# A decode step of attention and MLP: VectorE's program on a block border, and eight more matmuls on TensorE

## The chip, the cores and the metric

One Trainium2 chip, of which one core runs the kernel. The metric is device time in microseconds of one execution; the time of a kernel is the median of its runs. In the profile PE is TensorE's matmuls, PEld its weight loads, DVE VectorE, ACT ScalarE, POOL GpSimd and SP the engine whose queue issues nearly all DMAs here.

## The reference

Eight tokens (one for each batch entry, 576 wide) go through two branches that a gate mixes. Attention has 32 query heads on 16 key/value heads of 128, over the last 2048 of 8192 cached positions:

```python
x = A_x
g = _sigmoid((x * gate_w).sum(-1, keepdims=True))
# a: attention
q = (x @ wq).reshape(B, Sq, Hq, Dh).transpose(0, 2, 1, 3)
k = jnp.repeat(k_cache[:, :, Sk - W:, :], rep, axis=1)
v = jnp.repeat(v_cache[:, :, Sk - W:, :], rep, axis=1)
scores = jnp.einsum("bhqd,bhkd->bhqk", q, k) * (Dh ** -0.5)
p = _softmax(scores, axis=-1)
o = jnp.einsum("bhqk,bhkd->bhqd", p, v)
a = o.transpose(0, 2, 1, 3).reshape(B, Sq, Hq * Dh) @ wo
# b: MLP
h = _gelu(jnp.einsum("bsd,df->bsf", _layernorm(x), w1) + b1)
b = jnp.einsum("bsf,fd->bsd", h, w2) + b2
return g * a + (1 - g) * b
```

All inputs are bf16. The K and V windows are 64 MiB each; with the weights the kernel reads 154 MB.

## The kernel before, in words

The whole kernel is a plan: every operation is put in with `add` or `dma` (an engine, a function that emits the instructions, what it waits for, an estimated cost), `P.schedule()` orders the operations of each engine by these estimates, and `P.emit` then writes one engine's program after the other, with semaphore waits where another engine's work or a DMA is needed. `deps` are waited for; `after` only sets the order. The instructions that the framework puts ahead of each engine's program are there before the first `emit`.

Work is staged by what the DMA queue of SP brings, in this order: `wq`, `w1`, then 16 units of K and V of 4 MiB each, alternating, through four slots of SBUF, and at the end `M0`, `W0`, `W1`, `M1` of the list `stream`: two thirds of `w2`, the two halves of `wo`, and the last third of `w2` in three pieces of 8, 3 and 1 rows of blocks. A load is issued when its slot is free.

For each unit VectorE turns K around in four transposes (L719), TensorE makes the scores in PSUM banks 0 to 3 (on top of a mask that four matmuls of the constants `mrow` and `mcol` write there), VectorE takes the maximum (L643), ScalarE the exponential (L647), VectorE and ScalarE lay the probabilities out in blocks, and TensorE multiplies them with V in a loop on registers (L188). Four units make a group, whose parts VectorE scales and adds; `sel_x` and `oT` then bring the group's output into the form in which `wo` takes it. The last unit's V product is in bank 0.

The output is gathered in bank 7 (`BK_ACC`). A group of matmuls into it is an `AccGroup` (L567): one pair of matmuls (L576) of 8 columns for each block of 128 rows of `wo` or `w2`, one for each half of the 576 output columns. `wo_chunk(i)` (L829) loads half of `wo` and makes the group `proj0` or `proj1` of 16 pairs; `m2_chunk` (L845) makes the groups of `w2`. The list `o_m2` holds them in the order of their making, and each has the one before it in its `after`, so TensorE takes them in the order of `stream`. At the end VectorE (L883) and ScalarE (L884) copy one half each out of bank 7, and two DMAs write the output.

`held_matmul` (L174) emits a matmul that uses the weights which the matmul before it loaded.

Of the kernel before, what the change touches and what calls it, by code (L numbers as in the profile page):

```python
# [38 lines left out]
class _Plan:  # L39
# [10 lines left out]
    def add(self, eng, fn, deps=(), name=None, cost=0.1, after=(), prio=0):  # L50
        op = _Op(eng, fn, deps, name, cost, after=after, prio=prio)
        op.idx = len(self.all)
        self.all.append(op)
        return op

    def dma(self, eng, fn, semkey, nbytes, deps=(), name=None, after=(), prio=0):
        op = _Op(eng, fn, deps, name, self.DMA_ISSUE, after=after, is_dma=True, dma_sem=semkey, nbytes=nbytes, prio=prio)
        op.idx = len(self.all)
        self.all.append(op)
        return op  # L60
# [113 lines left out]
def held_matmul(nc, e, out, lhsT, rhs, start=False, stop=True, skip=False, tile_size=(128, 128), tile_position=(0, 0)):  # L174
    return e.add_instruction(mybir.InstMatmult(  # L175
        name=nc.get_next_instruction_name(), engine=mybir.EngineType.PE,
        ins=[e.lower_ap(rhs), e.lower_ap(lhsT)], outs=[e.lower_ap(out)],
        start_tensor_calc=start, stop_tensor_calc=stop, is_transpose=False, bass_skip_group_check=skip,
        tile_size=tile_size, tile_position=tile_position, ldweights=False))
# [15 lines left out]
def build_kernel(nc, A_x, A_k_cache, A_v_cache, A_wq, A_wo, B_x, B_w1, B_b1, B_w2, B_b2, gate_w, out):  # L195
# [29 lines left out]
    with ExitStack() as es:  # L225
# [79 lines left out]
        def view(name, parts=128):  # L305
            o, n, dt = R[name]
            a = arena[0:parts, o // 2: o // 2 + (n * (2 if dt == BF else 4)) // 2]
            if dt == F32:
                a = a.bitcast(F32)
            return a  # L310
# [5 lines left out]
        mrow, mcol = view("mrow"), view("mcol")  # L316
# [34 lines left out]
        def slot(s):  # L351
            return RAW[:, s * DE:min((s + 1) * DE, ND * DE + WOR * D)]
# [8 lines left out]
        def col(i, parts=128):  # L361
# [3 lines left out]
        ps = es.enter_context(nc.psum_tensor("ps", [128, 8, 512], F32))  # L365
# [13 lines left out]
        add, dma = P.add, P.dma  # L379
# [4 lines left out]
                                                        fill=0.0, base=0, channel_multiplier=1), deps=[o_ones], name="ident", cost=0.3)  # L384
        o_idf = add("pool", lambda e: e.tensor_copy(idf8, ident[0:8, 0:8]), deps=[o_ident], name="idf8", cost=0.15)
        o_r8 = add("pool", lambda e: e.tensor_copy(r8.rearrange("p (k b) -> p k b", b=8), bass.AP(arena_f, offset=foffs("idf8"), ap=[[AST // 2, 8], [0, 16], [1, 8]])),
                   deps=[o_idf], name="r8", cost=0.2)
# [5 lines left out]
                                                     fill=0.0, base=0, channel_multiplier=-1), deps=[o_ones], name="maskR", cost=0.8, prio=-1)  # L393
        o_mrow = add("pool", lambda e: e.affine_select(out=mrow, in_=zeros_bf, pattern=[[0, 8], [1, 8], [0, 2]], compare_op=ALU.is_equal,
                                                       fill=-BIG, base=0, channel_multiplier=-1), deps=[o_z], name="mrow", cost=0.3, prio=-1)
        o_mcol = add("pool", lambda e: e.affine_select(out=mcol, in_=ones_bf, pattern=[[0, 16], [1, 8], [0, 4]], compare_op=ALU.is_equal,
                                                       fill=0.0, base=0, channel_multiplier=-1), deps=[o_ones], name="mcol", cost=0.8, prio=-1)
# [23 lines left out]
        for s in range(2):  # L421
            o_xz.append(add("dve", (lambda s=s: lambda e: e.tensor_copy(xz[:, s, :].rearrange("p (k z) -> p k z", z=2)[:, :, s], x_sb[:, 512:576]))(),  # L422
                            deps=dx + [o_xz0], name="xz%d" % s, cost=0.12))
# [12 lines left out]
        for s in range(2):  # L436
            o_yz.append(add("dve", (lambda s=s: lambda e: e.tensor_copy(yz[:, s, :].rearrange("p (k z) -> p k z", z=2)[:, :, s], y_bf[:, 512:576]))(),
                            deps=[o_y, o_yz0], name="yz%d" % s, cost=0.12))
# [91 lines left out]
        for he in range(4):  # L530
            def fn(e, he=he):
                src = bass.AP(ps, offset=BK_SEL * 512 + 8 * he, ap=[[PST, 128], [1, 8], [32, 32]])
                return e.activation(out=q4[:, he, :, :], in_=src, func=ACTF.Copy)
# [49 lines left out]
        NU = NG * NT  # L583
# [14 lines left out]
        exp_done, sp_done, pv_done, mx_done = {}, {}, {}, {}  # L598
# [4 lines left out]
        def take_slot():  # L603
            n = n_slot[0]
            n_slot[0] += 1
            return (1, 2, 0, 3)[n % ND]
# [222 lines left out]
        def wo_chunk(i):  # L829
            s = ND if i == 0 else take_slot()  # L830
            dst = slot(s)[:, 0:WOR * D].rearrange("p (j c) -> p j c", j=WOR)
            src = A_wo.rearrange("(p j) c -> p (j c)", j=WOP)[:, WOR * D * i:WOR * D * (i + 1)]
            d = dma("sp", lambda e: e.dma_start(slot(s)[:, 0:WOR * D], src), "s%d" % s, WOR * 128 * D * 2, deps=slot_free[s], name="d_wo%d" % i, after=last_dma[-1:])
            last_dma.append(d)
            mms = [(oT[:, WOR * i + j, :], dst[:, j, :]) for j in range(WOR)]
            slot_free[s] = [AccGroup("proj%d" % i, mms, [oT_done[n] for n in range(NG)] + [d], cost=2.4, prio=2, after=o_m2[-1:]).op]
            o_m2.append(slot_free[s][0])

        o_m2, o_bias = [], []

        def bias(i):
            d = dma("act", lambda e: e.dma_start(b2_sb, B_b2.partition_broadcast(8)), "b2", 8 * D * 2, name="d_b2", after=[d_b1])
            o_bias.append(AccGroup("m2_b", [(ob[:, 0:8], b2_sb), (ob[:, 8:16], b2_sb)], [d, o_obl, o_obh], cost=0.6, after=[o_hp]).op)
# [20 lines left out]
        for kind, i in stream:  # L864
            {"K": k_item, "V": v_item, "W": wo_chunk, "M": m2_chunk, "B": bias}[kind](i)
# [21 lines left out]
        add("sp", lambda e: e.sem_inc(eng_sems["sp"], 1), deps=fin, name="final_wait", cost=0.05)  # L887

        P.schedule()
        for eng, handle in (("sp", nc.sync), ("act", nc.scalar), ("pool", nc.gpsimd), ("dve", nc.vector), ("pe", nc.tensor)):  # L890
            P.emit(eng, handle, eng_sems, dma_sems)

# [3 lines left out]
def bass_gated_mix__sliding_block_cached__mixer_channel_mlp__decode_kernel(  # L896
    nc: bass.Bass,
    A_x: bass.AP,
    A_k_cache: bass.AP,
    A_v_cache: bass.AP,  # L900
    A_wq: bass.AP,
    A_wo: bass.AP,
    B_x: bass.AP,
    B_w1: bass.AP,
    B_b1: bass.AP,
    B_w2: bass.AP,
    B_b2: bass.AP,
    gate_w: bass.AP,
    out: bass.AP,
):  # L910
    build_kernel(nc, A_x, A_k_cache, A_v_cache, A_wq, A_wo, B_x, B_w1, B_b1, B_w2, B_b2, gate_w, out)
# [28 lines left out]
```

## Time and profile before

| | before |
|---|---|
| median of 3 runs | 365.51 us (364.80 to 365.84) |
| the profiled execution | 365.76 us, of which the span from the first to the last instruction is 364.3 us |
| busy: PE, PEld, DVE, ACT, POOL | 293.8, 125.8, 237.3, 166.7, 26.4 us |
| DMA | 154.48 MB, mean 424 GB/s over the span |
| mean granted clock of TensorE | 0.963 |
| matmul instructions | 1944 |
| code fetched by DMA within the span | 8 packets of 16 KB (queue q8), 3 of 8 KB (queue q14) |

The page's strip of 40 slices gives the busy share of each engine over time, the granted clock (PEclk, in tenths of full speed) and the share of the 16 DMA engines that is busy. The chain of waits follows the last instruction back to what released it. The trace also keeps each DMA packet (start, length, size, queue), the landing events of each transfer, of which there are 16, one for each DMA engine, and the stretches of time in which each clock was granted. Times of single records count from the first instruction of the span.

### The profile page before, as it was taken

What the parts mean: (1) busy time and instruction counts of PE and PEld (TensorE: products, weight loads), DVE (VectorE), ACT (ScalarE), POOL (GpSimd) and SP (SyncE); (2) the same over time, 40 slices, a digit from 0 to 9 for tenths busy, and PEclk for the clock granted to TensorE, in tenths of its full rate; (3) what the DMA queues carried; (4) which work ended last, traced back from release to release, by engine and by line L of the source; (5) the groups of instructions that cost most, each with busy time, mean ns of one, the idle gap of its engine ahead of it and who ended that gap; (6) DMA issues with size and microseconds to landing.
All of it is one profiled execution on the core that took longest, in us unless ns stands there. A gap on an engine that the chain in (4) does not pass through costs nothing.

```text
span 364.3 us, 4853 instructions
## 1 busy us (share of the span) xinstructions
PE 293.8 (81%) x1944; PEld 125.8 (35%) x1420; DVE 237.3 (65%) x218; ACT 166.7 (46%) x122; POOL 26.4 (7%) x53
## 2 busy tenths in 40 slices
PE   0356544999999989999999798979797899979865
PEld 0201000253443524342525143423334160607643
DVE  0722976667768796858496868577585858396710
ACT  1012108373838483828383828281828365563000
POOL 9320070000010000000100000000000000003000
PEclk9976696999999999999999999999999999999998
DMA  8999999999999999999999999999999999999995
GB/s 348 433 428 412 457 407 454 407 457 407 457 412 453 425 439 428 431 435 428 446 417 444 417 450 414 457 412 450 410 453 417 447 423 439 425 439 425 432 418 208
DMA packets 6147, 154.48 MB, mean 424 GB/s; under 512 B 716, under 2 KB 884, under 8 KB 1272
## 3 DMA queue, kind: packets, MB, share of 16 engines
q1 hardware_dynamic: 6064, 154.28, 98.4%
q8 instruction: 8, 0.13, 0.1%
q10 hardware_dynamic: 72, 0.04, 0.1%
q14 instruction: 3, 0.02, 0.0%
HBM read 154.31 MB, written 0.01 MB: 424 GB/s over the span
## 4 chain that ended last, share of the span: by engine, by line
DMA 42%; DVE 36%; PE 13%; issue 7%; ACT 1%; ACTq 0%; POOL 0%
DMA arena<-in_A_k_cache_dram 32%; DVE arena L719 26%; DMA arena<-in_A_wo_dram 8%; PE ps L175 6%; DVE arena L643 4%; PE ps L188 2%; DMA arena<-in_gate_w_dram 2%; DVE arena L666 2%; PE ps L732 2%; PE ps L576 1%; PE ps L498 1%; DVE arena L795 1%; DVE arena L559 1%; DVE arena L554 0%; ACT arena L647 0%
## 5 line engine op out<-in xcount | busy, mean ns | idle before, releaser
L719 DVE STREAM_TRANSPOSE arena<-arena 128x2048 f32<-128x2048 f32 x64 | 143.3, 2281 | 14.4 <-DMA arena<-in_A_k_cache_dram 11.9
L175 PE MATMUL ps<-arena 128*128 128x512 bf16 (+3 forms) x524 | 132.2, 397 | 0.0
L672 ACT ACTIVATE arena<-arena 32x2048 bf16<-32x2048 bf16 x60 | 114.5, 1908 | 20.8 <-DVE arena L666 19.7
L188 PE MATMUL ps<-arena 128*128 x840 | 102.6, 275 | 3.4 <-issue 0.9
L188 PEld LDWEIGHTS ps<-arena 128*128 x840 | 81.7, 97 | 23.2 <-issue 10.1
L732 PE MATMUL ps<-arena 128*128 128x512 bf16 x128 | 51.0, 399 | 34.1 <-DVE arena L719 32.4
L732 PEld LDWEIGHTS ps<-arena 128*128 128x128 bf16 x128 | 12.4, 97 | 147.7 <-DVE arena L719 98.3
L644 ACT ACTIVATE arena<-arena 128x1 f32<-128x1 f32 x16 | 3.2, 203 | 114.3 <-DVE arena L643 114.3
L643 DVE TENSOR_REDUCE arena<-ps 128x1 f32<-128x2048 f32 x16 | 36.7, 2291 | 28.7 <-PE ps L175 28.7
L666 DVE STREAM_TRANSPOSE arena<-arena 128x1024 f32<-128x1024 f32 x15 | 18.7, 1245 | 37.5 <-ACT arena L647 37.5
L647 ACT ACTIVATE arena<-ps,arena 128x2048 bf16<-128x2048 f32 x16 | 40.6, 2535 | 0.5
L753 PE MATMUL ps<-arena 128*128 128x256 bf16 x184 | 25.3, 273 | 0.9 <-DMA arena<-in_A_v_cache_dram 0.9
L753 PEld LDWEIGHTS ps<-arena 128*128 128x128 bf16 x184 | 16.6, 100 | 13.3 <-issue 8.8
L576 PE MATMUL ps<-arena 128*8 128x288 bf16 (+1 forms) x140 | 11.1, 319 | 6.0 <-DMA arena<-in_A_wo_dram 5.1
L741 POOL MEMSET arena<- 128x4096 f32 x1 | 3.5, 3512 | 151.6 <-PE ps L175 151.6
L626 POOL COPY arena<-arena 32x64 bf16<-32x64 bf16 x16 | 3.7, 229 | 130.5 <-PE ps L175 122.9
L884 ACT ACTIVATE arena<-ps 8x288 bf16<-8x288 f32 x1 | 0.4, 401 | 27.5 <-PE ps L576 27.5
L449 PE MATMUL ps<-arena 8*128 8x8 bf16 x8 | 0.5, 170 | 15.0 <-DVE arena L422 10.2
L683 PE MATMUL ps<-arena 128*128 128x512 bf16 x16 | 6.5, 407 | 6.5 <-ACT arena L647 5.2
L576 PEld LDWEIGHTS ps<-arena 128*8 128x8 bf16 (+1 forms) x140 | 6.6, 95 | 11.1 <-DMA arena<-in_A_wo_dram 3.6
L795 DVE SCALAR_TENSOR_TENSOR arena<-ps,arena 128x128 f32<-128x128 f32 x28 | 9.3, 334 | 1.7 <-PE ps L753 1.3
L883 DVE CAST arena<-ps 8x288 bf16<-8x288 f32 x1 | 0.4, 445 | 14.1 <-PE ps L576 14.1
(103 smaller groups left out, 90.6 us busy)
## 6 DMA issues: line engine op xcount, KB each, us to landing
arena<-in_A_k_cache_dram SPq DMA_DIRECT2D x16, 4096.0 KB, 29.0
arena<-in_A_v_cache_dram SPq DMA_DIRECT2D x16, 4096.0 KB, 27.4
arena<-in_B_w_dram SPq DMA_DIRECT2D x1, 4608.0 KB, 23.7
arena<-in_A_wo_dram SPq DMA_DIRECT2D x2, 2304.0 KB, 31.1
arena<-in_A_wq_dram SPq DMA_DIRECT2D x1, 4096.0 KB, 13.4
arena<-in_B_w_dram SPq DMA_DIRECT2D x1, 3456.0 KB, 27.7
arena<-in_B_w_dram SPq DMA_DIRECT2D x1, 1152.0 KB, 22.6
arena<-in_B_w_dram SPq DMA_DIRECT2D x1, 576.0 KB, 24.6
```

The source lines that it names most:

```text
L175: return e.add_instruction(mybir.InstMatmult(name=nc.get_next_instruction_name(), engine=mybir.EngineType.PE, ins=[e.lower_ap(rhs), e.lowe ...
L188: return e.add_instruction(mybir.InstMatmult(name=nc.get_next_instruction_name(), engine=mybir.EngineType.PE, ins=[rhs, lhsT], outs=[e.low ...
L576: ins = e.matmul(ps[32 * j:32 * j + 8, BK_ACC, 0:JN], lhsT, rhs[:, JN * j:JN * j + JN], start=False, stop=True, skip_group_check=True, til ...
L643: mx = add("dve", lambda e: e.tensor_reduce(out=k(g, MX + x), in_=scores, axis=AXL.X, op=ALU.max), deps=[qk_unit[t]], name="mx%d" % t, cos ...
L647: ex = add("act", lambda e: e.activation(out=bass.AP(arena, offset=aoffs("P"), ap=[[AST, 128], [64, 32], [1, 2], [2, 32]]), in_=ps[:, 0:4, ...
L666: pc = add("dve", lambda e: e.transpose(view("PC").bitcast(F32), view("P").bitcast(F32)), deps=[ex] + (sp_done[t - 1][0] if t else [o_acc0 ...
L672: return e.activation(out=bass.AP(arena, offset=32 * a * AST + aoffs(home) + 64 * a, ap=[[AST, 32], [256, 32], [1, 64]]), in_=bass.AP(aren ...
L683: mm = e.matmul(*args, start=True, stop=False, skip_group_check=True) if n == 0 else held_matmul(nc, e, *args, start=True, stop=False, ski ...
L719: tr = add("dve", (lambda h=h, kb=kb, r2=r2: lambda e: e.transpose(bass.AP(arena_f, offset=foffs("KT") + kb * 2048, ap=[[AST // 2, 128], [ ...
L732: mm = e.matmul(*args, start=False, stop=True, skip_group_check=True) if rc == 0 else held_matmul(nc, e, *args, stop=True, skip=True)
L753: return e.matmul(dst, bass.AP(arena, offset=aoffs(home) + 256 * q + ee, ap=[[AST, 128], [2, 128]]), slot(s).rearrange("p (r k d) -> p r k ...
L795: fn = lambda e, src=src, w=w: e.scalar_tensor_tensor(out=X[:, g % 2, :], in0=src, scalar=w, in1=X[:, g % 2, :], op0=ALU.mult, op1=ALU.add)
```

## The change

Two things are added, and nothing is taken away.

In `wo_chunk`, behind `proj0`, TensorE gets an operation `fill`: eight matmuls of the mask's constants `mrow` and `mcol`, 128 by 128 by 512, into banks 1, 2 and 3 in turn, which nothing reads any more by then. The first loads the weights, the other seven hold them. `fill` goes into `o_m2`, so it stands between `proj0` and `proj1`. It depends on the last unit's exponential, which was the last reader of these banks.

Ahead of the emission VectorE gets an `addr_align(128, max_nops=0)`: the next instruction on it, the first of the kernel's own, is placed at a multiple of 128 instructions of 64 bytes (8 KB), and a branch leads over the gap in place of a row of no-operations.

```diff
@@ wo_chunk(i)
             slot_free[s] = [AccGroup("proj%d" % i, mms, [oT_done[n] for n in range(NG)] + [d], cost=2.4, prio=2, after=o_m2[-1:]).op]
             o_m2.append(slot_free[s][0])
+            if i == 0:
+                filler("fill", 8, o_m2[-1:])
 
         o_m2, o_bias = [], []
+
+        def filler(name, n, after):
+            def fn(e):
+                mm = None
+                for i in range(n):
+                    args = (ps[:, 1 + i % 3, :], mrow, mcol)
+                    mm = e.matmul(*args, start=True, stop=True, skip_group_check=True) if i == 0 else held_matmul(nc, e, *args, start=True, stop=True, skip=True)
+                return mm
+            o_m2.append(add("pe", fn, deps=[exp_done[NU - 1], o_mrow, o_mcol], name=name, cost=0.21 * n, after=after))
@@ ahead of the emission
         P.schedule()
+        nc.vector.addr_align(128, max_nops=0)
         for eng, handle in (("sp", nc.sync), ("act", nc.scalar), ("pool", nc.gpsimd), ("dve", nc.vector), ("pe", nc.tensor)):
             P.emit(eng, handle, eng_sems, dma_sems)
```

## The prediction

> **What bounds the kernel now.** I read the page first, then the chain of waits from its end backwards, then the busy time by stretches of the last 18 us, then the trace's single records of packets, landings and matmuls.
>
> ```profile
> PEclk9976696999999999999999999999999999999998
> DMA  8999999999999999999999999999999999999995
> ...
> q8 instruction: 8, 0.13, 0.1%
> ...
> q14 instruction: 3, 0.02, 0.0%
> ```
>
> The 16 DMA engines are full from the second slice to the last but one; no compute engine is. The granted clock is whole through the middle and dips in the last slice. Two queues carry nothing but code: 8 packets of 16 KB on q8 and 3 of 8 KB on q14. The end of the chain of waits (start, length, what):
>
> ```profile
> 327.60 29.48 DMA arena<-in_A_wo_dram
> 357.07 0.04 issue
> 357.12 5.29 PE ps L576 x56
> 362.43 0.45 DVE arena L883
> ```
>
> The second block of `wo` lands at 357.07; from there 56 matmuls, 28 pairs, run to the end. The busy time of the tail by stretches (length, then busy time and count of PE, PEld, DVE, ACT, POOL, then clock, DMA share, GB/s):
>
> ```profile
> 351.60:353.90 2.30, 2.13 (x32) 1.43 (x32) 0.00 (x0) 0.00 (x0) 0.00 (x0) 1.00 0.91 385
> 353.90:357.10 3.20, 0.00 (x0) 0.00 (x0) 0.00 (x0) 0.00 (x0) 0.00 (x0) 1.00 0.99 420
> 357.10:359.00 1.90, 1.88 (x20) 1.19 (x22) 0.00 (x0) 0.00 (x0) 0.00 (x0) 0.62 0.95 392
> 359.00:361.00 2.00, 2.00 (x22) 1.11 (x18) 0.00 (x0) 0.00 (x0) 0.00 (x0) 0.50 0.47 181
> 361.00:362.40 1.40, 1.39 (x22) 0.81 (x18) 0.00 (x0) 0.00 (x0) 0.00 (x0) 1.00 0.00 0
> ```
>
> `proj0` runs to 353.9, TensorE stands idle 3.2 us, and then works at half clock while the last data land. The four landings that feed the tail are at 357.07 (`wo`, 16 pairs), 359.82 (8 pairs), 360.87 (3) and 361.25 (1). The clock records put half clock from 357.57 to 360.99; starts of pairs are 0.1225 us apart at full clock and 0.240 at half. So the tail is 4 pairs full, 14 half, 10 full, and its last matmul ends at 362.39, 1.14 us after the last landing. Two things set the end: when the slowest DMA engine delivers, and the clock at which TensorE consumes.
>
> **The eight matmuls.** They stand on TensorE between `proj0` and `proj1`. What they wait for (ScalarE's last exponential, two constants from GpSimd) was over before 341, and the banks 1 to 3 that they write have no reader left, so they add no wait. TensorE is free at 353.7. The same kind of matmul, the held ones of the mask, takes 0.68 us for three in the chain of waits, so eight take 8 x 0.22 = 1.8 us, to 355.5. The 3.3 us of waiting for `wo` hides them; at half clock they would end near 357.2, and only what passes the landing of `wo` would be paid, up to 0.5 us.
>
> Do they hold the clock? The clock's changes all lie on one grid of 3.413 us. I took the busy share of TensorE in each cell: the cell 354.16 to 357.57 has 0.13 and is followed by half clock, as are cells with 0.11, 0.26 and 0.41; the lowest from 70 us on that kept full clock has 0.49 (279.1). With the filler that cell holds 1.39 us of it and 0.45 us or more of `proj1`: 1.84 of 3.41, 0.54, on the keeping side. The grid may lie otherwise in another run; the largest hole with the filler is then 349.9 to 351.7, which is there now too, and a cell around it has at worst 0.46, between the known rows. At full clock with the same landings: `proj1` 357.12 to 359.08, then 359.87 + 8 x 0.1225 = 360.85, 360.92 + 3 x 0.1225 = 361.29, the last pair done 0.29 us later, at 361.58. That is 0.81 us less. Now the landings, not the matmuls, set the end.
>
> The Trainium skill (TensorE: Matmul & The Clock Gate, Part 1) says that the clock falls back after at least one idle window of about 3.4 us. Taken at its word it speaks against the filler: the gap here is 3.27 us between matmuls, so nothing would be lost now and nothing won, 0 in place of 0.81 us. The clock of 0.50 after a cell that was 13% busy decides against that reading.
>
> Could the filler push TensorE over another code border? TensorE's fetches come at 336.64 and 351.32, 258 instructions apart. Behind the last there are 177 to the end; some 10 more stay below 258. No cost.
>
> **VectorE's start at a border.** A branch is added, and VectorE reaches it before 2.0 us, while its first work begins at 9.46, after the DMA of `gate_w`. Without that cover a wait for code would be paid in full, but even then not at once by the end: K and V loads land 27 to 29 us after issue and follow each other at 9.66 us, so the queue holds over 17 us of work. On that count I put the branch at nothing.
>
> What moves is where the borders lie, and each has a fetch. VectorE runs 47 of its recorded instructions before the 8 KB fetch at 61.25 and 178 before that at 284.76: 131 apart, a block of 128 within what its queue runs ahead. (The third 8 KB fetch, at 147.17, fits ScalarE.) Each fetch goes to one DMA engine: at 284.76 it starts as one 32 KB packet ends, takes 0.309 us, and the 32 KB packet behind it takes 1.744 instead of 1.213. That engine loses 0.84 us. The landing events (16 for each transfer, one for each DMA engine) show who it was: up to 279.45 the last five engines are within 0.12 us of each other; from the landing at 289.67 on, one engine is alone behind the rest, by 0.53 us, and is still 0.42 behind at 357.07 and 0.45 behind at 361.25. By its place in the row it is the one that the fetch at 61.25 had hit, and it was 0.42 from last before. So two fetches of VectorE on one DMA engine hold the last landings 0.42 us behind eight others, each hit once by a 16 KB fetch.
>
> With the program at a border, the next block is asked for at the start, before some 2 us, where the DMA engines are not yet full, and the one behind it 128 instructions on, which is VectorE's work at 202 to 207 us. One of the two hits moves to where nothing queues; the engine would then end 0.84 - 0.42 us ahead of the eight, and these set the landings. Bounds: 0 if the fetch falls on another late engine or the start still costs a place in the queue, at most 0.84 if the eight gained too, a loss of up to 0.84 if a hit is added to one of the eight. I take 0.42, the row's own distance. The Trainium skill (Runtime: NRT & Kernel Launch, Instruction fetch mechanics) calls the cost of crossing a block "mostly hidden"; by it this term would be 0, and the packet of 1.744 us speaks against that.
>
> **The sum.** Landings at 356.65, 359.40, 360.45, 360.83: the three pairs run 360.50 to 360.87, the last pair ends at 361.17. 362.39 - 361.17 = 1.22 us, of which 0.81 is clock and 0.41 fetch. The profiled execution took 365.76 us, of which 364.3 is span; it goes to 364.54. That execution is 0.25 above the median of the runs, 365.51. Taking the same 1.22 from the median gives 364.29, which I forecast as 364.3. The lowest run, 364.8, is about what the sum gives for a grid that happens to spare the tail (365.76 - 0.81 = 364.95); from such runs only the fetch's part comes off, to 364.4.
>
> **Rivals.**
> Only the clock: the code fetch hits a late DMA engine again. For it: eight engines wait at 0.42 to 0.57 us. Against it: both earlier hits were on one engine. 365.51 - 0.81 = 364.7.
> Only the fetch: the filler is too little for the gate. With landings 0.42 earlier the tail has 7 pairs full, 14 half, 7 full, ending at 362.01, so 365.51 - 0.38 = 365.1. For it: 0.54 is not far from 0.49, and activity may be weighed otherwise than I do. Against it: `proj0`'s cell, 0.62 busy with only 8 columns filled, kept the clock. If the alignment is also without effect, nothing changes: 365.5.
> Slower: the branch ends the reading ahead, so that VectorE meets each later border without its block. The one near 205 us is covered by the queue's 17 us. The last border then lies about 30 instructions behind VectorE's end, in the closing part behind the span, where nothing covers it. Its price I bound by the 1.93 us between the first two code packets of the trace's opening; it decides from 1.22 us on: 364.29 + 1.93 = 366.2, and without the clock's 0.81, 367.0. Against it: the trace shows a fetch at 365.64 and no wait in the span that either border explains. The Trainium skill (Runtime: NRT & Kernel Launch, Instruction fetch mechanics) states that a taken branch to a page outside the current two forces a fetch before execution goes on. The target here is the next block, and no run yet shows such a branch.
>
> **How the numbers follow.** Both parts 0.60; only the clock 0.17; only the fetch or nothing 0.13; slower 0.07; a gain beyond the sum 0.03. The range takes in the first two, most of the third, and downward the lowest run less the whole 0.84 us, 363.9: from 363.8 to 365.3. What a measurement of this kernel can tell from no change is about 0.3%, 1.1 us, so faster means below 364.4. The likeliest case, 364.3 to 364.5, sits on that line: most of it and the gain beyond count as faster, 0.52; its rest and the partial cases as the same, 0.42; slower 0.06.
>
> **What would show it.** A held matmul group of eight behind `proj0`, clock 1.00 through 357 to 361, pairs 0.1225 us apart in the whole tail, and idle time of TensorE before the last three groups; the last landing about 0.42 us earlier, with no DMA engine alone at the end; 8 KB fetches near the start and near 205 us and none near 61 and 285. I am wrong if the clock still halves after 357, if one DMA engine is still alone behind the rest, or if time appears behind the span.

## The result, and the profile after

The changed kernel takes 365.06 us in the median of 22 runs (364.91 to 365.29); the kernel before takes 365.88 us in 22 runs beside it (364.80 to 367.07). The ratio is 0.998, with a 95% interval of 0.9972 to 0.9987: 0.8 us less, 0.2%. That is beyond the interval, but within the 0.3% that the prediction drew as its line. Forecast were 364.3 us and, at 0.52, a gain of over 0.3%.

The end of the chain of waits (start, length, what) no longer has a long run of matmuls in it:

```profile
337.12 22.70 DMA arena<-in_B_w_dram
359.87 1.74 PE ps L576 x24
361.63 0.45 DVE arena L894
```

Before, 56 matmuls ran without a break from 357.12 to the end. Now TensorE waits for each piece of `w2`, and only the 24 matmuls behind 359.87 are left in the chain. The busy time by the same stretches as before (length, then busy time and count of PE, PEld, DVE, ACT, POOL, then clock, DMA share, GB/s):

```profile
351.60:353.90 2.30, 2.13 (x32) 1.52 (x33) 0.00 (x0) 0.00 (x0) 0.00 (x0) 1.00 0.93 393
353.90:357.10 3.20, 1.67 (x7) 0.00 (x0) 0.00 (x0) 0.00 (x0) 0.00 (x0) 1.00 1.00 426
357.10:359.00 1.90, 1.88 (x32) 1.36 (x32) 0.00 (x0) 0.00 (x0) 0.00 (x0) 1.00 0.94 390
359.00:361.00 2.00, 1.38 (x23) 0.71 (x20) 0.00 (x0) 0.00 (x0) 0.00 (x0) 1.00 0.42 164
361.00:362.40 1.40, 0.58 (x10) 0.19 (x8) 0.45 (x1) 0.40 (x1) 0.00 (x0) 1.00 0.00 0
```

The filler takes 1.67 us of the stretch that was empty (seven of its eight matmuls are in the trace), and the clock, 0.62 and 0.50 here before, is 1.00 all through. `proj1`'s 32 matmuls are done in the third stretch, where 20 were. The single records give the last matmul's end as 361.58 in place of 362.39, and the same four landings as before to 0.01 us: 357.08, 359.82, 360.88 and 361.25. So the whole 0.80 us between the two profiled executions lies between the last landing and the last matmul; in these two executions the landings did not move.

The alignment does what it says. A compare-and-branch stands on VectorE at 0.83 us, and VectorE's next instruction is at 2.03, where it was at 2.02 before. The 8 KB code packets that were at 61.25 and 284.76 us are now at 3.52 and 206.09.

### The profile page after: what moved, and what is told of

Same layout as the page of the kernel before. It is cut to its first block, busy times and chain, and to the rows that moved or that the text cites. A ratio compares the mean times of both kernels' runs of the same rounds, so it can differ in the third digit from the quotient of the medians.

```text
span 363.5 us, 4845 instructions
## 1 busy us (share of the span) xinstructions
PE 293.1 (81%) x1934; PEld 125.1 (34%) x1421; DVE 237.5 (65%) x218; ACT 166.7 (46%) x122; POOL 26.4 (7%) x53
## 4 chain that ended last, share of the span: by engine, by line
DMA 40%; DVE 37%; PE 14%; issue 7%; ACT 1%; ACTq 0%; POOL 0%
DMA arena<-in_A_k_cache_dram 32%; DVE arena L719 26%; PE ps L175 7%; DMA arena<-in_B_w_dram 6%; DVE arena L643 4%; DMA arena<-in_gate_w_dram 2%; PE ps L188 2%; PE ps L732 2%; DVE arena L666 2%; PE ps L753 1%; PE ps L498 1%; DVE arena L795 1%; DVE arena L559 1%; PE ps L576 0%; DVE arena L554 0%
## 5 line engine op out<-in xcount | busy, mean ns | idle before, releaser
L175 PE MATMUL ps<-arena 128*128 128x512 bf16 (+3 forms) x527 | 135.2, 398 | 9.8 <-DVE arena L719 7.1
L732 PE MATMUL ps<-arena 128*128 128x512 bf16 x126 | 50.8, 403 | 26.6 <-DVE arena L719 24.7
L576 PE MATMUL ps<-arena 128*8 128x288 bf16 (+1 forms) x140 | 9.7, 286 | 4.8 <-DMA arena<-in_A_wo_dram 3.3
L576 PEld LDWEIGHTS ps<-arena 128*8 128x8 bf16 (+1 forms) x140 | 5.8, 86 | 10.3 <-DMA arena<-in_A_wo_dram 3.2
L554 DVE TENSOR_TENSOR arena<-arena 128x1152 f32<-128x1152 f32 x1 | 1.4, 1357 | 10.2 <-ACT arena L552 10.2
```

The lines of the kernel that those rows point to most:

```text
L175: return e.add_instruction(mybir.InstMatmult(name=nc.get_next_instruction_name(), engine=mybir.EngineType.PE, ins=[e.lower_ap(rhs), e.lowe ...
L576: ins = e.matmul(ps[32 * j:32 * j + 8, BK_ACC, 0:JN], lhsT, rhs[:, JN * j:JN * j + JN], start=False, stop=True, skip_group_check=True, til ...
L732: mm = e.matmul(*args, start=False, stop=True, skip_group_check=True) if rc == 0 else held_matmul(nc, e, *args, stop=True, skip=True)
```

## The experiments

Theory A: all of the gain is the clock of the tail, and the alignment, which moves two code packets without sparing a DMA engine either, nets nothing. Its rivals were that the alignment has a part in the gain (B, D) or takes from it (C). The runs were made in three groups, each on a chip of its own and with its own runs of the kernel before, so a kernel is compared through its ratio to those. Across groups such a comparison is coarse: the median of the kernel before was 365.45, 365.66 and 365.66 us, and the ratio of one and the same kernel, the eight matmuls alone, was 0.9986 in the first group and 0.9976 in the second.

**The two parts, one at a time** (first group, the kernel before at 365.45 us):

```diff
-        nc.vector.addr_align(128, max_nops=0)      # e1: the eight matmuls alone
```
```diff
-            if i == 0:                             # e2: the alignment alone
-                filler("fill", 8, o_m2[-1:])
```

> The eight matmuls alone, without the alignment. Theory A (all of the gain is the clock of the tail; the alignment moves two code packets but both still hit one DMA engine in a full queue, so it nets nothing): as the changed kernel, 365.06 us within 0.1, clock 1.00 behind 357, last matmul ending near 361.58, last landing 361.25. Theory B (clock and alignment each bring part of the 0.82 us): 365.4. Theory C (the alignment costs some 0.4 us and the clock brings 1.2): 364.6.

> The alignment alone, without the eight matmuls. Theory A: as the kernel before, 365.88 us in the median and as scattered (364.9 to 366.1), half clock from a point behind 356, 8 KB packets near 3.5 and 206, last landing 361.25. Theory B: 365.4. Theory C: 366.3.

The matmuls alone took 364.90 us (364.77 to 364.99), ratio 0.9986 (0.9977 to 0.9994). Their profile has the clock whole where the kernel before has 0.62 and 0.50 (columns as above):

```profile
357.10:359.00 1.90, 1.88 (x32) 1.18 (x26) 0.00 (x0) 0.00 (x0) 0.00 (x0) 1.00 0.98 405
359.00:361.00 2.00, 1.40 (x22) 0.82 (x22) 0.00 (x0) 0.00 (x0) 0.00 (x0) 1.00 0.46 177
```

The alignment alone took 365.38 (364.62 to 366.71), ratio 0.9997 (0.9985 to 1.001): it changes neither the median nor the scatter. The profiled execution of the alignment alone, one of 366.57 us, shows why the kernel before scatters upward (columns as above):

```profile
353.30:356.80 3.50, 0.25 (x5) 0.00 (x0) 0.00 (x0) 0.00 (x0) 0.00 (x0) 0.83 0.97 413
356.80:359.00 2.20, 2.19 (x20) 1.25 (x22) 0.00 (x0) 0.00 (x0) 0.00 (x0) 0.50 0.94 388
359.00:361.00 2.00, 2.00 (x20) 1.14 (x18) 0.00 (x0) 0.00 (x0) 0.00 (x0) 0.50 0.41 159
361.00:363.20 2.20, 2.13 (x24) 1.08 (x18) 0.03 (x1) 0.03 (x1) 0.00 (x0) 0.68 0.00 0
```

The last landing is at 360.94, but half clock lasts from 355.59 to 362.42, two cells of the prediction's grid (stretches of 3.413 us), and the last matmul ends at 363.13. The 22 runs of before fall into three heaps that fit no, one and two lost cells: four up to 365.12, fifteen from 365.46 to 366.08, three from 366.83 on. In the 22 runs beside them, with the eight matmuls, no run is above 365.29, and in the profile of every kernel here with eight or sixteen the tail's clock is whole. Not all scatter is the clock's: the changed kernel run again (below) reaches 365.65 us, and the profile of that run has a whole clock in the tail but its last landing at 361.75, 0.50 us later than in the first profile.

**How many matmuls it takes.**

```diff
-                filler("fill", 8, o_m2[-1:])
+                filler("fill", 2, o_m2[-1:])       # e3, alignment kept; e4: 16; e13: 4 without the alignment
```

> Two matmuls in place of eight, alignment kept: TensorE is busy 0.43 us in the gap in place of 1.7. If the clock goes by the busy share of a cell of 3.413 us: the cell of the gap holds at most 0.43 + 0.45 = 0.26 of its length in a placing like that of the profiled execution of before, so half clock again in most executions, 365.6 to 365.9 us and scattered. If it is enough to break up the idle stretch of 3.3 us (what is left is 2.9 without a matmul): 365.06, not scattered.

> Four matmuls alone. They end near 354.8 and leave 2.3 us idle ahead of 357.1. By the busy share of the cell: a cell that holds all of it is 0.33 busy and loses the clock, one that holds up to 1.9 us of it keeps it, so about half of the executions near 365.0 and the rest between 365.3 and 365.9. If breaking the idle stretch is enough: all near 365.0.

> Sixteen matmuls in place of eight, alignment kept: they take 3.46 us and end near 357.5, 0.4 us behind the landing of the second block of wo. Theory A: proj1 starts 0.4 us later and ends near 359.5, still before the next landing at 359.82, so 365.06 unchanged. If the tail were bound by TensorE also at full clock: 365.4.

Two took 365.57 us, ratio 1.0 (0.9992 to 1.0009): no gain, with one run of 12 at 364.79. Four took 365.69, ratio 0.9994 (0.998 to 1.0009): three of 12 runs lie at 365.09 to 365.16, the other nine from 365.42 to 365.90. Breaking the idle stretch is therefore not enough; how much of a cell is filled decides. Nor is it the length of an idle stretch: with the offset of 96 (e5, below) TensorE stood idle for 2.79 us up to 243.82, a border of the grid cut this into two cells, 0.64 and 0.54 busy, and the clock stayed; with two matmuls 1.80 us of idleness up to 282.00 lay in one cell of 0.47, and half clock followed. I had expected half of the runs with four to be spared, so my model of the placing is only roughly right. The profile with two has the clock at 0.61 and 0.56 where eight have 1.00:

```profile
353.30:356.90 3.60, 0.80 (x8) 0.10 (x1) 0.00 (x0) 0.00 (x0) 0.00 (x0) 1.00 0.96 410
356.90:359.00 2.10, 2.10 (x22) 1.30 (x24) 0.00 (x0) 0.00 (x0) 0.00 (x0) 0.61 0.98 409
359.00:361.00 2.00, 2.00 (x22) 1.12 (x18) 0.00 (x0) 0.00 (x0) 0.00 (x0) 0.56 0.49 188
```

Sixteen took 364.68 us, ratio 0.9974 (0.9962 to 0.9986). They push `proj1` back, and nobody waits for it:

```profile
353.66 3.40 PE L175 MATMUL ps<-arena 128*128 128x512 bf16 x15
...
356.99 1.81 PEld L576 LDWEIGHTS ps<-arena 128*8 128x8 bf16 x32 [3.46 <-DMA arena<-in_A_wo_dram]
356.99 2.13 PE L576 MATMUL ps<-arena 128*8 128x288 bf16 x32
359.50 0.83 PEld L576 LDWEIGHTS ps<-arena 128*8 128x8 bf16 x16 [0.70 <-DMA arena<-in_B_w_dram]
```

In this timeline (start, length; in brackets how long the engine stood idle before, and what ended that) `proj1` starts at 356.99 although its data landed at 356.71; TensorE still waits at 359.50 for `w2`.

**Was the 0.2 us of sixteen over eight the alignment?** Sixteen with the alignment had taken 0.22 us less than eight without it, on one chip. The second group (the kernel before at 365.66 us) had the changed kernel, sixteen without the alignment, and eight without it once more. The edits are those above.

> The changed kernel itself, on the chip of this call. Theory A (alignment nets nothing): within 0.1 us of the eight matmuls alone. Theory D (alignment brings a little): 0.15 to 0.25 us less than those.

> Sixteen matmuls without the alignment; with it they took 364.68 us where eight without it took 364.90 on the same chip. If the 0.2 us came from the longer filler: 0.2 less than the eight alone. If from the alignment: the same as the eight alone.

> The eight matmuls alone once more, on the chip of this call: the base for the other three. 364.9 us within 0.15.

The changed kernel took 365.12 us (364.84 to 365.65), ratio 0.9972 (0.9957 to 0.9987); sixteen alone 365.01 (364.82 to 365.38), 0.9977 (0.9963 to 0.9991); eight alone 365.01 (364.88 to 365.15), 0.9976 (0.9963 to 0.9989). Neither the longer filler nor the alignment brings the 0.2 us back. Where they came from in the first group stays open, for sixteen with the alignment were not run again; apart from them no version here is faster than eight matmuls alone.

**What a code packet costs.** Two experiments were to add one of VectorE's packets to the full queue. The first was a failure of mine:

```diff
-        nc.vector.addr_align(128, max_nops=0)
+        nc.vector.addr_align(128, offset=96, max_nops=0)      # e5
```

> The eight matmuls, and VectorE's program placed 96 instructions behind a border in place of on it: borders then come after 32 and 160 of its instructions, near 22 to 34 us and 267 us, besides the packet that the branch brings near 3 us, so three packets of 8 KB of VectorE in the full queue in place of two. If each costs its DMA engine 0.84 us and that engine is already among the last: last landing and time 0.7 to 0.84 us later than with the alignment to the border in the same call (some 365.5 to 365.7 on a chip where that gives 364.8). If the packets have nothing to do with the last landing: no difference.

It took 365.09 us, ratio 0.9975 (0.9961 to 0.9989). But its packets are at 18.10 and 236.50: two, not three, and none near 3 us. Position 96 seems to lie in the block in which the program starts anyway, so the branch enters no new block. It tells nothing about a third packet. Its trace does show the price of one: behind the packet at 236.50 the last DMA engine, until then level with the next, lands 0.89 us after it. The second did it with instructions:

```diff
+        req("pad", 128, F32)
...
-        nc.vector.addr_align(128, max_nops=0)
+        for i in range(128):
+            nc.vector.memset(view("pad", 8)[:, i:i + 1], 0.0)      # e9, with the eight matmuls
```

> The eight matmuls without the alignment, and 128 tiny writes of VectorE (8 elements each, to memory that nothing uses) ahead of its program, so that it crosses one border more, near 4 to 8 us: three packets of 8 KB in the full queue in place of two, near 5, 62 and 285 us. If VectorE's packets all go to one DMA engine, which is among the last, and cost it 0.84 us each: last landing and time later by 0.5 to 0.84 us, 365.5 to 365.85 where the eight alone take 365.0. If code packets do not set the last landing: 365.0. VectorE's own start some 3 to 8 us later costs nothing if the 17 us in the queue cover it.

It took 365.78 us where the kernel before took 365.66 (third group), ratio 0.9995 (0.9983 to 1.0007); against the 0.9976 of the eight alone that is 0.0019 of 365.66, 0.7 us more. The eight alone were not run in this group, and by their 0.9986 of the first group it would be 0.3 us, so the trace is the firmer evidence. The page's queue of 8 KB code packets (packets, MB, share) shows the additional one, and the chain ends accordingly later:

```profile
q14 instruction: 4, 0.03, 0.0%
```
```profile
338.08 22.61 DMA arena<-in_B_w_dram
360.70 0.04 issue
360.74 1.75 PE ps L577 x24
```

The last piece but two of `w2` is there at 360.70, 0.88 us later than in the changed kernel. The clock of the tail is whole. From the landing events and packets (us; the gap is from the last of the 16 DMA engines to the next one, at the last landing):

```
kernel                       VectorE's packets      last landing  gap
before                       61.25, 284.76          361.25        0.45
eight alone (e1)             62.19, 284.49          360.98        0.08
sixteen alone (e7)           62.49, 284.79          361.28        0.18
eight alone again (e8)       62.49, 284.79          361.28        0.39
four alone (e13)             61.32, 284.83          361.32        0.15
changed                      3.52, 206.09           361.25        0.25
alignment alone (e2)         3.17, 205.79           360.94        0.17
two, alignment (e3)          3.12, 205.79           361.03        0.08
sixteen, alignment (e4)      3.05, 205.65           360.89        0.09
changed again (e6)           3.48, 206.17           361.75        0.23
eight, offset 96 (e5)        18.10, 236.50          361.40        0.74
eight, 128 writes (e9)       7.80, 62.14, 284.45    362.14        1.43
```

With three packets one engine stands 1.43 us behind all others, and the end moves with it. The landings show when: this gap goes from 0.18 to 0.80 us at the packet at 62.14 and from 0.60 to 1.52 at the one at 284.45, so both fell on the engine that was already last. So VectorE's code does go to one DMA engine here, and this engine does set the end when it is hit often enough. The alignment moves the packets but not the last landing: its mean is 361.22 us over the five kernels without and 361.17 over the five with it.

**Is a packet free ahead of the full queue?** This is the step of the prediction on which the alignment's gain hung. Both kernels let SP's first large DMA wait for a fill of GpSimd that ends near 5 us; e11 has the alignment and e12 has not.

```diff
-        d_wqr = dma("sp", ..., "wq", 64 * 8192, name="d_wqr")
+        d_wqr = dma("sp", ..., "wq", 64 * 8192, deps=[o_qz], name="d_wqr")
```

> Eight matmuls and alignment, and the first large DMA of SP waits for a GpSimd fill that ends near 5.0 us, so the queue fills some 4.2 us later, behind VectorE's first packet near 3.3 us. The prediction's step was that a packet ahead of the full queue is free. If so: one hit in place of two, and 0.2 to 0.45 us less than the same late start without the alignment, with no DMA engine alone at the end. If not: the same. Both near 369.2 us.

> The same late start with the eight matmuls and without the alignment: 365.0 + 4.2 = 369.2 us, with VectorE's packets near 62 to 66 and 285 to 289 us in the full queue. The base for the one before.

They took 368.76 us with and 368.74 without the alignment, both with a ratio of 1.0073 (1.0056 to 1.009 and to 1.0091). VectorE's first packet was at 1.98 with the alignment, well ahead of the first packet of `wq` at 6.09, and the second at 210.12; without it they were at 66.09 and 288.39. At the landing of the first part of `wq` the last engine is 0.17 us behind the next with the alignment and 0.14 without: ahead of the full queue the packet sets no engine apart. The last landings are at 364.89 and 365.02, 0.13 us apart, which is less than two executions of one kernel differ (360.98 and 361.28 for the eight alone), and the medians are the same. The expected 0.2 to 0.45 us did not come, because in these two executions the engine with two packets is not alone at the end at all: the gap is 0.06 without the alignment and 0.03 with it. What sparing a packet brings where its engine is alone at the end is therefore not shown.

## Why the prediction was right or wrong

**The clock, 0.81 us: right in mechanism and size.** The profiled execution lost 0.80 us, by the steps that were written down: half clock gone, the same landings, groups waiting for their data at 359.87 and 360.92, last matmul ending at 361.58. The filler ended near 355.7 and cost nothing. That the two profiled executions agree in their landings to 0.01 us is luck: other executions of kernels with two packets have the last one anywhere from 360.89 to 361.75. The Trainium skill (TensorE: Matmul & The Clock Gate, Part 1) makes an idle window of about 3.4 us the condition for losing the clock; the runs show it lost after cells of 0.13 (before), 0.18 (two matmuls) and 0.40 busy (alignment alone) and kept after 0.46 (the changed kernel, 349.29), so the fill of the cell is what counts. The border is not sharp: over all traces here, from 60 us on and by recorded matmul time, five of the 27 cells between 0.43 and 0.49 busy lost the clock, the others and all above kept it. The prediction's 0.54 for the filled cell is above that band; its worst placing of 0.46 lies within it.

**The code packet, 0.41 us: wrong.** The step that failed is "the next block is asked for at the start, before some 2 us, where the DMA engines are not yet full". The branch ran at 0.83, but its packet started at 3.52, and the packets of `wq` run from 1.85 on. Even with the late start, where no packet of `wq` is there yet, the code packet comes only at 1.98. At the landing at 5.27 of the first part of `wq` one engine is 0.84 us behind the next; over the five kernels with the alignment this gap is 0.57 to 0.84 us, over the five without it 0.03 to 0.17. Two hits moved, and none was spared: the last landing stayed at 361.25 where 360.83 was forecast. The rival "only the clock" described the outcome, though for another reason: not another late engine, but a start that "still costs a place in the queue", which the prediction had as its lower bound.

The size of the term was not safe either. The 0.42 us by which one engine stood behind the others was read from one execution; over the kernels with two packets this gap is 0.08 to 0.74, and with the late start it is 0.03 and 0.06. Where each engine stands early on may make much of the difference, which was not tried; one trace cannot show that the gap is the same in others.

**What was right about code.** That VectorE's packets fall on one engine was an inference from the order of the landings; e9 showed it for two of its three. That the price of one is 0.84 us held: behind the packets at 206.09, 236.50 (e5) and 284.45 (e9) stands a 32 KB packet of 1.744 us, as at 284.76 before, and the last piece but two of `w2` comes 0.88 us later in e9 than in the changed kernel. In the median of e9 it is some 0.7 us, with the reservation made there. The positions, near the start and near 205 us, came out at 3.52 and 206.09. The Trainium skill (Runtime: NRT & Kernel Launch, Instruction fetch mechanics) calls the crossing of a block mostly hidden; it is hidden from VectorE, which in the changed kernel shows no wait for it at 206, but not from a DMA engine in a full queue.

**The base.** The sum took 0.25 us off for the profiled execution's distance to a median of three runs. In 22 runs that median is 365.88, above the profiled execution: three runs of a kernel with three heaps are too few for this. Against 365.88 the clock's 0.80 gives 365.08, and 365.06 was measured. That this fits so well is partly luck: what the median gains depends on how many executions of the kernel before lose no, one or two cells, and in the other groups the eight matmuls alone took 0.55 and 0.65 us off it.

**Slower.** The branch cost VectorE nothing at the start, and no time appeared behind the span: 365.0 of the profiled execution against 363.5 of its span is 1.5 us, as before.

## What to carry to other kernels

Where the last work waits for the last data, look at the granted clock there: an idle stretch ahead of it can halve the clock for just those matmuls, and a filler that the wait hides takes this time away, and the scatter that comes from the clock, if it fills enough of the cell (here eight matmuls did; with four the clock was spared in three runs of twelve). Code is traffic too: in this kernel, which the DMA engines bound, a block that VectorE's program crosses cost one DMA engine 0.84 us, the packet's 0.31 and 0.53 of the packet behind it, so count the packets and see on whom they fall before borders are moved. And a gap between DMA engines that one trace shows needs a second execution before a gain is counted on it.

## What the runs showed of the hardware that was not expected

- Half clock can outlast a cell that is well used. With the alignment alone the cell 355.59 to 359.00 was 0.64 busy, at half clock, and the next was still at half; only after a cell of 1.00 did the clock return, at 362.42. The same 0.62 to 0.66 of a cell keeps a clock that is whole (in the kernel before at 350.75 and 258.59).
- From the branch to its code packet it took 2.7 us (0.83 to 3.52) where the packets of `wq` ran from 1.85 on, and 1.15 us (0.83 to 1.98) where they began at 6.09. So more than half of the 2.7 us is due to the queue, if nothing else differs between the two.
- A queue that filled 4.2 us later (first packet of `wq` at 6.08 in place of 1.86) cost the eight matmuls alone only 3.5 us: ratio 1.0073 against 0.9976, from two groups with the same median of before. From that packet to the last landing it is 358.94 us in place of 359.42. With the late start the 16 landings of the first part of `wq` lie within 0.34 us and those of the second within 0.42; without it the second's spread over 1.20. What makes the early disorder was not tried; the small loads of `x`, the gate and the biases, which then no longer fall among the large packets, are the nearest suspects.
